# First layer of the experts by eleven block products in place of twelve, with token groups in pairs outside and experts inside

## The chip, the cores and the metric

The kernel runs on one core of a Trainium2 chip. The metric is the device time of one execution in microseconds. A core has five engines that run their own instruction streams in order and wait for each other on semaphores: TensorE (PE, with its weight loads shown as PEld), VectorE (DVE), ScalarE (ACT), GpSimd (POOL) and SyncE (SP, which here only issues DMAs).

## The reference

A delta-rule attention gives x with 3072 tokens and 384 columns. A mixture of 8 experts follows, each a first layer of 384 by 1024, a relu and a second layer of 1024 by 384, weighted per token by P, and last a block of four matrices, two of them side by side with a product by element.

```python
def _moe_ref(x, w_gate, w1, w2):
    ...
    out = np.zeros((N, D), dtype=np.float32)
    for e in range(E):
        h = np.maximum(x @ w1[e], 0.0)
        ye = h @ w2[e]
        out += P[:, e:e + 1] * ye

def _moe2_ref(x, w1, w2, w3, w_out):
    a = x @ w1
    b = x @ w2
    h = a * b @ w3
    return (h @ w_out).astype(np.float32)
```

## The kernel before

All matrices of the mixture and of the last stage are fp32. Each operand is split into a high and a low part, and a product of 128 rows by 128 columns takes three matmuls (high by high, high by low, low by high) that add up in one PSUM bank.

**Order.** The program hands every operation to a class `Plan` with the tiles that it reads and writes, a priority and a cost for each engine that may take it. `Plan` simulates the engines with these costs and so writes one fixed order for each engine; where two engines may take an operation (POOL or DVE for most subtractions) it chooses one. A DMA costs its bytes by 300 GB/s plus 0.9 us there. PSUM banks and buffers are rings that hand out a slot when the last user is done.

**Attention stage.** It runs over 12 chunks of 256 tokens. Expert 0 of a chunk is computed there as well (`e0`), for the first ten chunks.

**Expert stage (`phase_b`).** All 3072 tokens' x, in high and low parts, lie in SBUF (`xT` for five groups of 512 tokens, `xr` for the sixth), and so does `acc`, the weighted sum of all groups. The outer loop runs over 14 half experts (experts 1 to 7, each as two sets of four blocks of 128 hidden columns, after what is left of expert 0), the inner over the six groups. For one half expert and one group PE does 4 blocks x 9 matmuls of 512 columns (first layer, one PSUM bank a block), then 3 x 12 (second layer, one bank for each 128 output columns). ACT writes relu of a block as its high part (L966), DVE the low part with one `scalar_tensor_tensor` (L335), both into a slot of `hA` or `hB`; of these there are five, so that PE may be one block ahead of the second layer. DVE multiplies a second-layer bank by the spread weight `pb` into `tmp` and adds `tmp` to `acc` (L332; POOL may take the sum).

**Weights.** A block of weights (`load_w`, L811) is 384 x 128 of w1 and 128 x 384 of w2, which makes 128 x 768 in a slot of `rawB` (two slots, two DMAs of 192 KB each). ACT copies it to the high part in `wA` (128x768, L325), DVE or POOL subtracts for the low part (128x768, L332). `wA` has eight slots, one for each block of an expert: while one half is used the other is loaded. Since the groups run inside, a set of four blocks is loaded once in six groups.

**Conversion.** The last stage's matrices arrive as 64-bit floats. `convert` turns them into high and low fp32 parts in DRAM (`w_d`), 256 columns a job, in the gaps of the expert stage: six operations on DVE, two on ACT, and one or two that POOL or DVE takes, and DMAs in and out.

**Last stage (`phase_c`).** `xT` is reused: four of its parts for the two first matrices (high and low), the fifth as three slots through which w3 streams, issued on POOL's queue. w3 and w_out are first multiplied with each other (`m34`: 16 pieces of 12 matmuls of 384 columns, each needs 512 KB of w3). Then come 12 chunks of 256 tokens: split of x into high and low (`x2` in `xr`), 16 products of 9 matmuls of 256 columns, the product by element, its split, and 2 x 24 matmuls of 384 columns into the output.

## Time and profile before

| | |
|---|---|
| median of 3 runs | 2250.84 us (2250.38 to 2253.55) |
| the profiled execution | 2248.74 us |
| its span in the trace | 2247.0 us |
| mean granted clock | 0.98 |
| PE busy | 2172.9 us, 97% |
| DVE busy | 1222.3 us, 54% |
| ACT busy | 569.9 us, 25% |
| POOL busy | 187.7 us, 8% |

The span is what the trace covers, from the first to the last instruction; the profiled execution lies 1.74 us above it, the median of the runs 3.84 us. Busy shares are averages over three stages that differ: attention ends near 540 us of the span, the expert stage near 1915 us, the rest is the last stage.

### The profile page before, as it was taken

The numbers are of one execution on the slowest core, as the hardware profiler recorded it, in microseconds if no ns is written. First come the engines' busy times: TensorE is split into PE (matmuls) and PEld (weight loads), VectorE is DVE, ScalarE is ACT, GpSimd is POOL, SyncE is SP. The second block draws the span as 40 slices with busy tenths as digits, with TensorE's granted clock in tenths as the row PEclk, the third lists the DMA queues.
The fourth block names the chain that finished last, engine by engine and source line by source line (L and its number), as shares of the span: only waits on it lengthen the run. The fifth ranks groups of instructions, "written<-read, shape, count | busy, mean of one in ns | idle before, by whom it ended". The sixth has DMA issues, their size and how long they took to land.

```text
span 2247.0 us, 40062 instructions
## 1 busy us (share of the span) xinstructions
PE 2172.9 (97%) x17133; PEld 1900.9 (85%) x17133; DVE 1222.3 (54%) x2147; ACT 569.9 (25%) x1144; POOL 187.7 (8%) x200
## 2 busy tenths in 40 slices
PE   2999999989999999999999999999999999999999
PEld 2999999977888888888888888888888888999999
DVE  8667756768777777776444444444444444223332
ACT  3333233332222222322112121121211111233332
POOL 3000000023211011110000000000000001200000
PEclk6999999999999999999999999999999999999999
DMA  5331232055333232322101010100101043500000
GB/s 193 94 101 57 64 94 61 24 158 171 95 107 111 80 111 86 116 89 85 43 19 43 15 47 15 46 30 28 47 15 32 17 155 85 107 19 15 15 15 22
DMA packets 134691, 153.13 MB, mean 68 GB/s; under 512 B 10608, under 2 KB 105008, under 8 KB 133744
## 3 DMA queue, kind: packets, MB, share of 16 engines
q1 hardware_dynamic: 115632, 128.80, 18.7%
q0 software_dynamic: 18880, 21.76, 3.8%
q8 instruction: 134, 2.20, 0.4%
q14 instruction: 45, 0.37, 0.1%
HBM read 119.23 MB, written 31.29 MB: 67 GB/s over the span
## 4 chain that ended last, share of the span: by engine, by line
PE 91%; DMA 3%; DVE 2%; issue 1%; ACT 1%; POOL 0%; SPq 0%; DVEq 0%; ACTq 0%; POOLq 0%
PE b L321 91%; DMA kt<-in_kT 1%; DMA xs_d<-xst 1%; ACT g L325 1%; DMA xst<-xs_d 0%; POOL wA L332 0%; DVE acc L332 0%; DMA wraw<-in_moe_w 0%; DMA yr<-in_moe_w 0%; DMA pb<-p_d 0%; DMA kraw<-in_k 0%; ACT tt L325 0%; SPq L352 0%; DVE p L335 0%; DVE p L332 0%
## 5 line engine op out<-in xcount | busy, mean ns | idle before, releaser
L321 PE MATMUL b<-xT,wA 128*128 128x512 f32 x2520 | 588.2, 390 | 0.0
L321 PEld LDWEIGHTS b<-xT,wA 128*128 128x128 f32 x2520 | 473.0, 188 | 102.4
L321 PE MATMUL b<-hA,wA 128*128 128x512 f32 (+1 forms) x2304 | 496.1, 357 | 2.2 <-DVE hA L335 1.3
L321 PEld LDWEIGHTS b<-hA,wA 128*128 128x128 f32 x2304 | 383.0, 190 | 70.9 <-DVE hA L335 2.7
L321 PE MATMUL b<-hB,wA 128*128 128x512 f32 (+1 forms) x1584 | 416.2, 390 | 0.0
L321 PEld LDWEIGHTS b<-hB,wA 128*128 128x128 f32 x1584 | 294.2, 189 | 64.4
L332 DVE TENSOR_TENSOR tmp<-b,pb 128x512 f32<-128x512 f32 x252 | 174.0, 691 | 255.4 <-PE b L321 254.6
L966 ACT ACTIVATE hA<-b 128x512 fp32r<-128x512 f32 (+1 forms) x176 | 103.4, 587 | 647.1 <-PE b L321 647.0
L335 DVE SCALAR_TENSOR_TENSOR hA<-b,hA 128x512 fp32r<-128x512 f32 (+1 forms) x216 | 146.8, 680 | 178.2 <-ACT hA L966 166.5
L321 PE MATMUL b<-xr,wA 128*128 128x256 f32 (+1 forms) x1368 | 233.6, 325 | 2.4 <-ACT wA L325 2.1
L321 PEld LDWEIGHTS b<-xr,wA 128*128 128x128 f32 x1368 | 201.7, 191 | 25.0 <-ACT wA L325 2.6
L321 PE MATMUL b<-xr,xT 128*128 128x256 f32 x1728 | 209.9, 283 | 0.0
L321 PEld LDWEIGHTS b<-xr,xT 128*128 128x128 f32 x1728 | 209.3, 192 | 0.0
L335 DVE SCALAR_TENSOR_TENSOR hB<-b,hB 128x512 fp32r<-128x512 f32 (+1 forms) x176 | 119.2, 678 | 151.9 <-ACT hB L966 151.7
L332 DVE TENSOR_TENSOR acc<-acc,tmp 128x512 f32<-128x512 f32 x250 | 180.5, 722 | 6.5
L966 ACT ACTIVATE hB<-b 128x512 fp32r<-128x512 f32 (+1 forms) x176 | 102.9, 585 | 215.8 <-PE b L321 202.2
L332 DVE TENSOR_TENSOR cv<-b,cv 128x256 f32<-128x256 f32 x96 | 40.7, 424 | 163.5 <-PE b L321 162.9
L332 POOL TENSOR_TENSOR wA<-rawB,wA 128x768 fp32r<-128x768 f32 x17 | 36.7, 2157 | 674.9 <-ACT wA L325 674.9
L332 POOL TENSOR_TENSOR cv<-cv 128x256 f32<-128x256 f32 (+1 forms) x68 | 52.5, 772 | 304.0 <-DVE cv L1063 177.4
L325 ACT ACTIVATE cvs<-cv 128x256 fp32r<-128x256 f32 x72 | 29.0, 402 | 167.0 <-DVE cv L335 166.9
L325 ACT ACTIVATE wA<-rawB 128x768 fp32r<-128x768 f32 x56 | 45.8, 841 | 73.6 <-PE b L321 39.9
L321 PE MATMUL b<-wA,hB 128*128 128x384 f32 x288 | 56.5, 337 | 0.0
(137 smaller groups left out, 1783.2 us busy)
## 6 DMA issues: line engine op xcount, KB each, us to landing
pb<-p_d SPq DMA_DIRECT2D x90, 256.0 KB, 3.2
rawB<-in_moe_w SPq DMA_DIRECT2D x112, 192.0 KB, 3.2
w_d<-cvs SPq DMA_DIRECT2D x112, 128.0 KB, 2.5
cvr<-in_w3T SPq DMA_DIRECT2D x32, 256.0 KB, 3.2
xT<-w_d POOLq DMA_DIRECT2D x32, 256.0 KB, 3.4
kt<-in_kT SPq DMA_DIRECT2D x12, 512.0 KB, 5.2
qt<-in_qT SPq DMA_DIRECT2D x12, 512.0 KB, 4.7
cvr<-in_moe_w SPq DMA_DIRECT2D x24, 256.0 KB, 3.2
```

Of the source, the lines that this page charges most:

```text
L321: self.nc.tensor.matmul(*args, skip_group_check=True, **kw)
L325: self.nc.scalar.activation(out=out, in_=in_, func=AF.Copy, **({} if scale is None else {"scale": scale}))
L332: self.E[eng].tensor_tensor(out=out, in0=in0, in1=in1, op=op)
L335: self.nc.vector.scalar_tensor_tensor(out=out, in0=in0, scalar=scalar, in1=in1, op0=op0, op1=op1)
L966: g.op({"ACT": act(N, True)}, lambda e, s=s, h=h, hx=hx, N=N: nc.scalar.activation(out=self.hv(h, hx, N)[:, 0], in_=self.ps(s, N), func=AF ...
```

## The change

The expert stage is turned round. Three passes run outside, each over one pair of token groups (0 and 1, 2 and 3, 4 and 5); inside run the 14 half experts. So there are 42 units of one half expert and two groups. Expert 0 is computed for all 12 chunks in the attention stage.

Within a unit the four blocks are taken in two pairs (`q`). The first layer of a pair of blocks and a pair of groups is a 2 x 2 array of blocks by three blocks of x's columns: 12 block products before. Two of the three columns now go by Winograd's scheme of seven products in place of eight, and the third adds its four: 11 products, 33 matmuls of 512 columns in place of 36. Sums and differences of x blocks (`forms`, nine operands a pass, high and low) are made once a pass; sums and differences of weight blocks are made in every unit by `load_pair`, which takes the place of `load_w`. A pair of blocks is loaded into both slots of `rawB`; ACT copies 768 and 640 columns, DVE or POOL subtracts as many; then five sums of 128 columns are made in place in `rawB`, and 256, 256 and 128 columns of results are copied (ACT) and subtracted (DVE or POOL) into `wS` and the free corner of `wA`. Only then are the two slots free for the next pair. Weights are loaded once for two groups in place of six: 84 pairs, 168 blocks, in place of 56 blocks.

The seven steps of a pair run in three PSUM banks X, Y, Z. After steps 0, 2 and 3 the partial sum in a bank is needed by itself: `hold` has ACT copy it to a buffer `rt` (four slots), while PE goes on adding to the bank or to another. After steps 1, 4 and 5 `done` has DVE add a bank to the held sum, ACT write the relu from `rt` (L1009), and DVE the low part from `rt`. Step 6 goes as all blocks went before, straight from PSUM (L1027). Steps of the two pairs alternate. A second layer of 2 x 3 x 12 matmuls of 512 columns follows, the second group first.

Sums over experts are kept for two groups. They are written to DRAM (`xf_d`) after the first and second pass and read again in the last stage; expert 0's part is added in the unit of expert 4 (`add_first`).

The conversion runs by 128 columns a job (136 jobs in place of 72). The last stage runs by six groups of 512 tokens, in the order 4, 5, 0 to 3, with 9 matmuls of 512 in place of 18 of 256; w3 streams through two, later three, slots in `wS`, and the first group's x goes to `wS` when all of m34 has been done.

```diff
+    def load_pair(self, e_, h, q, prio):
+
+        nc, g, T, a = self.nc, self.g, self.T, self.a
+        r0 = ["w1open", "x11"]
+        n1 = 8 * e_ + 4 * h + 2 * q
+        ps = 2 * h + q
+        raws = []
+        both = {"POOL": pool2(768), "DVE": dve(768)}
+        for j, n in enumerate((n1, n1 + 1)):
+            f, sl = n % 8, n % 8
+            raw = self.rawB.new()
+            raws.append(raw)
...
+            c0 = 128 * j
+            m = 768 - c0
+            g.op({"ACT": act(m)}, lambda e, n=n, rv=rv, c0=c0: self.copy("ACT", self.wb(n)[:, c0:768], rv()[:, c0:768]),
+                 r=[(raw, 0), (raw, 1)], w=[("w", sl, 0)], prio=prio)
+            g.op({"POOL": pool2(m), "DVE": dve(m)}, lambda e, n=n, rv=rv, c0=c0: self.tt(
+                e, self.wb(n)[:, 768 + c0:1536], rv()[:, c0:768], self.wb(n)[:, c0:768].bitcast(F32), ALU.subtract),
...
+        def sub(out, i0, i1, op, m=1):
+
+            g.op({"POOL": pool2(128), "DVE": dve(128)}, lambda e: self.tt(e, k(*out), k(*i0), k(*i1), op), r=[], w=[(r1, 0), (r2, 0)], prio=prio)
...
+        sub((r2, 1), (r2, 0), (r2, 1), ALU.add)
+        sub((r2, 0), (r1, 0), (r2, 0), ALU.subtract)
+        sub((r1, 0), (r2, 1), (r1, 0), ALU.subtract)
+        sub((r1, 1), (r1, 1), (r1, 0), ALU.subtract)
+        sub((r1, 2), (r1, 2), (r2, 2), ALU.subtract)
...
+        for m, src, dst, key in ((256, lambda: T["rawB"][:, r1.at, 0:256], lambda i: ws(i), lambda i: ("wS", ps, i, 0)),
+                                 (256, lambda: T["rawB"][:, r2.at, 0:256], lambda i: ws(i, 256), lambda i: ("wS", ps, i, 1)),
+                                 (128, lambda: T["rawB"][:, r1.at, 256:384], lambda i: self.wb(n1 + 1)[:, 768 * i:768 * i + 128], lambda i: ("w", sl2, i))):
+            g.op({"ACT": act(m)}, lambda e, src=src, dst=dst: self.copy("ACT", dst(0), src()), r=rk + ["bopen"], w=[key(0)], prio=prio)
+            g.op({"POOL": pool2(m), "DVE": dve(m)}, lambda e, src=src, dst=dst: self.tt(e, dst(1), src(), dst(0).bitcast(F32), ALU.subtract),
+                 r=rk + [key(0)], w=[key(1)], prio=prio)
...
+    PASSES = ((0, 1), (2, 3), (4, 5))
...
+            M[-1] += ([("X", [(A11, 3)], True), ("Z", [(A12, 4), (A13, 5)], True), ("X", [(S2, 6)], False),
+                       ("Y", [(S1, 7), (A23, 1)], True), ("X", [(S3, 2)], False), ("Y", [(S4, 8), (S5, 1)], False),
+                       ("X", [(A22, 0), (A23, 5)], False)],)
...
+            def hold(nm, s):
+                t = temps[q, nm] = self.rt.new()
+                g.op({"ACT": act(512, True)}, lambda e: self.copy("ACT", T["rt"][:, t.at], self.ps(s, 512)), r=[s], w=[t], prio=pe)
...
+                g.op({"DVE": dve(512)}, lambda e: self.tt("DVE", tv(), self.ps(s, 512), tv(), ALU.add), r=[s], w=[t], prio=pe)
+                g.op({"ACT": act(512)}, lambda e: nc.scalar.activation(out=hv(0), in_=tv(), func=AF.Relu), r=[t], w=[(out, 0, 0)], prio=pe)
+                g.op({"DVE": dve(512)}, lambda e: self.stt(hv(1), tv(), 0.0, hv(0).bitcast(F32), ALU.max, ALU.subtract),
+                     r=[t, (out, 0, 0)], w=[(out, 1, 0)], prio=pe)
...
+            if step == 0:
+                hold("X1", X)
+            elif step == 1:
+                done("X1", Z, hq["11"])
+            elif step == 2:
+                hold("X2", X)
+            elif step == 3:
+                hold("Y1", Y)
+            elif step == 4:
+                done("Y1", X, hq["22"])
+            elif step == 5:
+                done("X2", Y, hq["12"])
...
+        for idx, (q, step) in enumerate(self.STEPS):
+            product(q, step, idx)
+        for s in (1, 0):
+            bl = [(M[q][3]["12" if s else "11"], M[q][4]) for q in range(2)] + [(M[q][3]["22" if s else "21"], M[q][4] + 1) for q in range(2)]
...
+    STEPS = [(q, s) for ss in ((0, 1), (2, 3), (4,), (5,), (6,)) for q in range(2) for s in ss]
...
-            self.open("xTp", "left", xT=((128, 5, 2, 4, 3, 128), F32R))
-            self.open("accp", "left", acc=((128, 6, 3, 512), F32))
-            self.open("hBp", "right", hB=((128, 5 - HA, 1024), F32R))
-            self.open("cvp", "right", cv=((128, 3, 256), F32), cvr=((128, 2, 512), F32))
-            self.open("cvs", "right", cvs=((128, 2, 256), F32R))
+            self.open("xTp", "left", xT=((128, 4, 2, 4, 3, 128), F32R))
+            self.open("accp", "left", acc=((128, 2, 3, 512), F32))
+            self.open("hBp", "right", hB=((128, HB, 1024), F32R), wS=((128, 4, 1024), F32R))
+            self.open("cvp", "right", cv=((128, 3, CN), F32), cvr=((128, 2, 2 * CN), F32), rt=((128, 4, 512), F32))
+            self.open("cvs", "right", cvs=((128, 2, CN), F32R))
...
-        units = [(0, range(EB, 8))] + [(e_, range(4 * h, 4 * h + 4)) for e_ in range(1, NE) for h in range(2)]
-        for u, (e_, fs) in enumerate(units):
...
+        units = [(p, e_, h) for p in range(3) for e_ in range(1, NE) for h in range(2)]
+        for n, (p, e_, h) in enumerate(units):
...
+            if (e_, h) == (1, 0):
+                self.forms(p, pr - .6)
...
+            if n + 1 < len(units):
+                for q in range(2):
+                    self.load_pair(*units[n + 1][1:], q, pr + .5)
+            self.unit(p, e_, h, pr, 250.0 + n / 100, pb)
+            if (e_, h) == (4, 0):
+                self.add_first(p, pr + .6)
+            if (e_, h) == (7, 1) and p < 2:
+                for s, ch in enumerate(self.PASSES[p]):
+                    self.dma(lambda ch=ch: T["xf_d"][ch], lambda s=s: T["acc"][:, s], 786432, [("acc", s, kk) for kk in range(3)], [("xf", ch)], 260 + n / 100)
...
-        n = 256
+        n = CN
...
-        w3ring = Ring(range(3))
+        w3ring = Ring([0, 1])
+        self.after("ws2", self.last_readers([("wS", 2, i, m) for i in range(2) for m in range(2)]), 2999, hook=lambda end: w3ring.free.append((end, 2)))
...
-        for c in range(12):
...
+        self.after("w3free", self.m34_ops, 2999, hook=lambda end: x2r.free.append((end, 1)))
+        x2 = lambda s, i: (T["xr"].rearrange("p i a h k n -> p (i a h k n)") if s.at == 0 else T["wS"][:, 0:3].rearrange("p a n -> p (a n)"))[
+            :, 1536 * i:1536 * i + 1536].rearrange("p (k n) -> p k n", k=3)
...
+        for ci, c in enumerate((4, 5, 0, 1, 2, 3)):
...
+                    g.op({"PE": 9 * .2267}, ab, r=xk + [k for v in wsrc.values() for k in v[1]], w=[sab[j], (h, "z", j)], prio=pc)
...
-                if full and c < 10:
+                if full:
```

How the order moves at three places. First ACT, in the middle of the expert stage. Before, this is where the copies of a set of weights (`wA<-rawB`, 768 columns) stand among the relus (`hA<-b`, `hB<-b`):

```order
L325 ACTIVATE wA<-rawB 128x768 x2
L1065 ACTIVATE cv<-cvr 128x256
L966 ACTIVATE hA<-b_128 128x512
L966 ACTIVATE hA<-b_130 128x512
L325 ACTIVATE wA<-rawB 128x768
L966 ACTIVATE hB<-b_133 128x512
L325 ACTIVATE cvs<-cv 128x256
L325 ACTIVATE wA<-rawB 128x768
L966 ACTIVATE hB<-b_129 128x512
```

After, in the seventh unit of the first pass, the end of the first layer (`hB<-rt` and `hA<-rt` are relus of held sums, `cv` and `cvs` belong to the conversion):

```order
L327 ACTIVATE wA<-rawB 128x128
L327 ACTIVATE rt<-b_133 128x512
L327 ACTIVATE cvs<-cv 128x128
L1009 ACTIVATE hB<-rt 128x512 x2
L327 ACTIVATE wA<-rawB 128x768
L1009 ACTIVATE hB<-rt 128x512
L327 ACTIVATE wA<-rawB 128x640
L1027 ACTIVATE hB<-b_130 128x512
L1198 ACTIVATE cv<-cvr 128x128
L1009 ACTIVATE hA<-rt 128x512
```

The copies of the second pair of the next unit's weights stand between the last four relus of this unit, and such a group stands in every unit; before it stands once in six groups.

Second DVE, at the same kind of place. Before:

```order
L332 TENSOR_TENSOR wA<-rawB,wA 128x768
L335 SCALAR_TENSOR_TENSOR hA<-b_128,hA 128x512
L335 SCALAR_TENSOR_TENSOR hA<-b_130,hA 128x512
L332 TENSOR_TENSOR wA<-rawB,wA 128x768
L335 SCALAR_TENSOR_TENSOR hB<-b_133,hB 128x512
L332 TENSOR_TENSOR wA<-rawB,wA 128x768
L335 SCALAR_TENSOR_TENSOR hB<-b_129,hB 128x512
```

After, in the thirteenth unit of the first pass (`rt<-b,rt` adds a bank to a held sum; the `rawB<-rawB` sum in the last row belongs to the second pair's weights):

```order
L334 TENSOR_TENSOR rt<-b_130,rt 128x512
L337 SCALAR_TENSOR_TENSOR hB<-rt,hB 128x512
L334 TENSOR_TENSOR rt<-b_131,rt 128x512
L337 SCALAR_TENSOR_TENSOR hB<-rt,hB 128x512
L1192 TENSOR_SCALAR cv<-cvr 128x128
L334 TENSOR_TENSOR wA<-rawB,wA 128x640
L337 SCALAR_TENSOR_TENSOR hA<-rt,hA 128x512
L337 SCALAR_TENSOR_TENSOR hB<-b_134,hB 128x512
L337 SCALAR_TENSOR_TENSOR cv<-cvr,cv 128x128
L337 SCALAR_TENSOR_TENSOR hB<-b_127,hB 128x512
L334 TENSOR_TENSOR rawB<-rawB 128x128
```

Six blocks of a unit have a sum ahead of their low part, and the low parts of the last blocks stand behind a subtraction of the second pair's weights.

Third PE, where the expert stage ends (`wA,xT` and `wA,wS` with 384 columns is m34, `xr,xT` and `wS,xT` the first products of the last stage, `hA`/`hB,wA` the second layer). Before:

```order
L321 MATMUL b_130<-hB,wA 128x512 x3
L321 MATMUL b_133<-wA,xT 128x384 x24
L321 MATMUL b_126<-wA,xT 128x384 x12
L321 MATMUL b_131<-xr,xT 128x256 x9
L321 MATMUL b_132<-xr,xT 128x256 x9
L321 MATMUL b_127<-xr,xT 128x256 x9
L321 MATMUL b_128<-xr,xT 128x256 x9
L321 MATMUL b_126<-wA,xT 128x384 x12
L321 MATMUL b_130<-wA,xT 128x384 x24
```

After:

```order
L323 MATMUL b_127<-hB,wA 128x512 x6
L323 MATMUL b_132<-wA,wS 128x384 x24
L323 MATMUL b_131<-wA,wS 128x384 x24
L323 MATMUL b_134<-wA,wS 128x384 x24
L323 MATMUL b_128<-wA,wS 128x384 x24
L323 MATMUL b_130<-wA,wS 128x384 x24
L323 MATMUL b_133<-wA,wS 128x384 x24
L323 MATMUL b_129<-wA,wS 128x384 x24
L323 MATMUL b_127<-wA,wS 128x384 x24
L323 MATMUL b_132<-wS,xT 128x512 x9
L323 MATMUL b_131<-wS,xT 128x512 x9
```

m34 was mixed with the first products of the last stage and stands now in one piece ahead of all of them.

## Rows read from the trace of the kernel before

**Rows 1.** The page: busy time of the engines over the whole span, and the granted clock of PE in 40 slices.

```profile
PE 2172.9 (97%) x17133; PEld 1900.9 (85%) x17133; DVE 1222.3 (54%) x2147; ACT 569.9 (25%) x1144; POOL 187.7 (8%) x200
...
PEclk6999999999999999999999999999999999999999
```

**Rows 2.** The chain of work that ended last: its last piece (start, us, what), and its shares by line.

```profile
540.67 1702.96 PE b L321 x8419
...
by line: PE b L321 91.5%; issue 1.3%; DMA kt<-in_kT 0.6%; DMA xs_d<-xst 0.6%; ACT g L325 0.5%; DMA xst<-xs_d 0.5%; POOL wA L332 0.4%; DVE acc L332 0.4%; DMA wraw<-in_moe_w 0.4%; DMA yr<-in_moe_w 0.3%; DMA pb<-p_d 0.2%; DMA kraw<-in_k 0.2%; 
```

**Rows 3.** Busy time in three stretches: the expert stage with conversion, the same without, and 10 us in which m34 and the first products of the last stage run. Columns: stretch, its length, busy us (instructions) of PE, PEld, DVE, ACT and POOL, granted clock, share of the DMA engines, GB/s.

```profile
700.00:1000.00 300.00, 300.00 (x1308) 245.05 (x1307) 218.25 (x474) 81.54 (x169) 48.29 (x60) 1.00 0.33 99
1000.00:1300.00 300.00, 300.00 (x1307) 245.10 (x1306) 146.97 (x234) 57.23 (x98) 11.54 (x10) 1.00 0.14 43
...
1920.00:1930.00 10.00, 10.00 (x71) 10.00 (x70) 1.88 (x5) 1.68 (x4) 5.04 (x7) 1.00 1.00 185
```

**Rows 4.** The timeline of PE in the expert stage, one group's turn from the second layer to the first and back. Columns: start us, us, engine, line, operation, tiles, shape, count. A row ends later than the next one begins, since the ends are modelled; a rate is taken from start to start.

```profile
1304.93 1.55 PE L321 MATMUL b<-hB,wA 128*128 128x512 f32 x6
...
1306.32 1.55 PE L321 MATMUL b<-hA,wA 128*128 128x512 f32 x6
...
1308.40 8.37 PE L321 MATMUL b<-xT,wA 128*128 128x512 f32 x36
...
1316.61 0.86 PE L321 MATMUL b<-hB,wA 128*128 128x512 f32 x3
```

**Rows 5.** The timeline of PE at the start of the last stage: m34 (384 columns) and first products (256 columns).

```profile
1906.19 6.41 PE L321 MATMUL b<-wA,xT 128*128 128x384 f32 x36
1912.44 4.47 PE L321 MATMUL b<-xr,xT 128*128 128x256 f32 x36
1916.75 6.41 PE L321 MATMUL b<-wA,xT 128*128 128x384 f32 x36
```

**Rows 6.** The timeline of the other engines around the handover of weights in the part without conversion; in brackets the idle time before an instruction and what ended it.

```profile
1306.55 0.69 DVE L332 TENSOR_TENSOR acc<-acc,tmp 128x512 f32<-128x512 f32 x1
...
1308.19 1.86 POOL L332 TENSOR_TENSOR wA<-rawB,wA 128x768 fp32r<-128x768 f32 x1 [97.43 <-ACT wA L325]
...
1309.33 1.27 DVE L332 TENSOR_TENSOR acc<-acc,tmp 128x512 f32<-128x512 f32 x1
1310.52 0.95 DVE L332 TENSOR_TENSOR wA<-rawB,wA 128x768 fp32r<-128x768 f32 x1
...
1311.50 8.79 SPq L352 DMA_DIRECT2D rawB<-in_moe_w  x8
...
1314.69 0.85 ACT L325 ACTIVATE wA<-rawB 128x768 fp32r<-128x768 f32 x1 [1.36 <-DMA rawB<-in_moe_w]
1315.45 0.58 ACT L966 ACTIVATE hB<-b 128x512 fp32r<-128x512 f32 x1
...
1317.51 0.85 ACT L325 ACTIVATE wA<-rawB 128x768 fp32r<-128x768 f32 x1 [1.48 <-DMA rawB<-in_moe_w]
```

**Rows 7.** The same handover in the part with conversion.

```profile
615.23 0.94 DVE L332 TENSOR_TENSOR wA<-rawB,wA 128x768 fp32r<-128x768 f32 x1
615.48 2.42 POOL L332 TENSOR_TENSOR wA<-rawB,wA 128x768 fp32r<-128x768 f32 x1 [0.73 <-ACT wA L325]
...
616.20 2.64 SPq L352 DMA_DIRECT2D rawB<-in_moe_w  x4
...
620.27 0.85 ACT L325 ACTIVATE wA<-rawB 128x768 fp32r<-128x768 f32 x1 [1.89 <-DMA rawB<-in_moe_w]
...
621.92 0.84 ACT L325 ACTIVATE wA<-rawB 128x768 fp32r<-128x768 f32 x1 [0.33 <-DMA rawB<-in_moe_w]
```

**Rows 8.** Groups of instructions by line, operation and shape: busy us, mean ns of one, idle time before them and what ended it.

```profile
L332 DVE TENSOR_TENSOR acc<-acc,tmp 128x512 f32<-128x512 f32 x250 | 180.5, 722 | 6.5
L332 DVE TENSOR_TENSOR tmp<-b,pb 128x512 f32<-128x512 f32 x252 | 174.0, 691 | 255.4 <-PE b L321 254.6
L335 DVE SCALAR_TENSOR_TENSOR hA<-b,hA 128x512 fp32r<-128x512 f32 x208 | 143.5, 690 | 173.5 <-ACT hA L966 161.7 <-ACT hA L777 10.8
...
L332 DVE TENSOR_TENSOR wA<-rawB,wA 128x768 fp32r<-128x768 f32 x39 | 38.2, 982 | 19.8 <-ACT wA L325 19.7
L332 POOL TENSOR_TENSOR wA<-rawB,wA 128x768 fp32r<-128x768 f32 x17 | 36.7, 2157 | 674.9 <-ACT wA L325 674.9
...
L335 DVE SCALAR_TENSOR_TENSOR cv<-cv 128x256 f32<-128x256 int32 x64 | 27.0, 422 | 2.5
L332 DVE TENSOR_TENSOR cv<-cv 128x256 f32<-128x256 f32 x63 | 26.6, 423 | 10.3 <-POOL cv L332 7.3 <-DVE cv L1063 0.5
L325 ACT ACTIVATE cvs<-cv 128x256 fp32r<-128x256 f32 x64 | 26.5, 414 | 148.9 <-DVE cv L335 148.9
...
L1071 DVE TENSOR_SCALAR cv<-cvr 128x256 int32<-128x256 int32 x64 | 20.8, 324 | 0.0
...
L332 POOL TENSOR_TENSOR cvs<-cv,cvs 128x256 fp32r<-128x256 f32 x26 | 19.6, 755 | 75.4 <-ACT cvs L325 75.4
L332 DVE TENSOR_TENSOR cvs<-cv,cvs 128x256 fp32r<-128x256 f32 x38 | 15.8, 417 | 2.9 <-ACT cvs L325 2.9
...
L332 DVE TENSOR_TENSOR cv<-cv 128x128 f32<-128x128 f32 x13 | 3.8, 292 | 0.8
...
L325 ACT ACTIVATE cvs<-cv 128x128 fp32r<-128x128 f32 x8 | 2.5, 310 | 18.1 <-DVE cv L335 18.0
```

More of the change, by code (lines that the diff above doesn't have):

```diff
@@ L31 @@
 NP = 2
+HB = 7
+CN = 128
 NTC = 2
@@ L883, in phase_b @@
         self.after("x11", [g.wr["xs", 11, b] for b in range(2)], -200)
-        for n in range(EB, 8):
-            self.load_w(n, self.rawB, raw_t, 300, r=["w1open", "x11"])
         def open_b(e):
@@ new lines, in phase_c @@
+        yv = lambda yb: T["yr"].rearrange("p s n -> p (s n)")[:, DM * yb.at:DM * yb.at + DM] if yb.at < 2 else T["tmp"][:, yb.at - 2, 0:DM]
+        for ci, c in enumerate((4, 5, 0, 1, 2, 3)):
+            pc = pr + 20 + ci
+            xb = x2r.new()
+            xs = lambda ci=ci: T["acc"][:, ci % 2]
+            ak = [("acc", ci % 2, kk) for kk in range(3)]
+            if ci > 1:
+                self.dma(xs, lambda c=c: T["xf_d"][c], 786432, [("xf", c)], ak, pc - 1.5)
+            ak = ak + ["x5free"]
+            g.op({"ACT": act(1536)}, lambda e, xb=xb, xs=xs: self.copy("ACT", x2(xb, 0), xs()), r=ak, w=[(xb, 0)], prio=pc)
+            g.op({"POOL": pool2(1536), "DVE": dve(1536)}, lambda e, xb=xb, xs=xs: self.tt(
```

362 lines of the change are left out of this document (198 added, 164 removed).

## The prediction

> **What bounds the kernel now.** I read the page's busy times first, then the chain, then stretches, then single turns. PE is busy for 97% of the span at the granted clock of its upper level, 2.4 GHz, after the first slice [rows 1]. The chain shows that this is no accident of averages: from 540.67 us on it is one piece of PE work of 1702.96 us [rows 2]. In the expert stage PE is busy for 300 of 300 us [rows 3]. So only fewer matmul columns help there, and any wait of PE is paid in full. The second reading is who has room to take on work. With conversion, DVE is busy for 218 of 300 us, without it for 147 [rows 3].
>
> **What leaves PE.** A first-layer matmul takes 8.21 us / 36 = 0.228 us from start to start, a second-layer one 1.39 / 6 = 0.2315 us [rows 4]. Each of 42 units loses 2 x 3 first-layer matmuls: 252 x 0.228 = 57.4 us. In the last stage 1728 matmuls of 256 columns take 4.31 / 36 = 0.1197 us each [rows 5], 206.8 us; as 864 of 512 columns at 0.228 they take 197.0, a gain of 9.8. m34 and the output products keep their columns. All of this lies on the path: **67.2 us**.
>
> **What is added outside the units.** Four terms, 20 us together.
> - m34 was mixed with other products and now runs in one piece. 12 matmuls of it take 6.25 / 36 x 12 = 2.08 us [rows 5] and eat 512 KB of w3; while w3 streams, the DMA engines are full at 185 GB/s [rows 3], so 512 KB take 2.83 us. 16 pieces need 45 us by DMA and 33 us by PE. Two or three pieces lie ready; but the loads of the second matrix (3.1 MB, 17 us by that rate) share the last second layer with them. I take +9, between 3 (all but four pieces hidden) and 16 (nothing ready).
> - The first group's x goes into `wS`, which m34 reads. So an ACT copy and a subtraction of 1536 columns stand between m34 and the next matmul: about twice 0.85 [rows 6] and twice 0.98 us [rows 8], +4 with the handovers.
> - The first unit: its weights must be summed before it starts, while expert 0's last chunks still use DVE and ACT: +3, between 0 and 8.
> - Two changes of pass: 9 copies and 13 DVE or POOL operations of 512 columns. PE's second layer of 72 x 0.2315 = 16.7 us covers them, but DVE has also 6 x (0.69 + 0.72) us of its sums [rows 8] and weights to do in it. +2 each, from 0 to 4.
>
> **What is added in a unit.** This decides the sign. A unit is now 66 x 0.228 + 72 x 0.2315 = 31.7 us of PE work. First the load on DVE, by the mean times of [rows 8]: 6 `tmp` at 0.691, 6 `acc` at 0.722, 6 sums into `rt` priced as `tmp`, 8 low parts at 0.690 give 18.1 us. Weights: the planner gave DVE per unit about 1.4 subtractions of 768 columns (0.98), 0.7 of 640 (about 0.85), 2.8 of 256 (0.417), 1.1 of 128 and 4.7 sums of 128 (0.292): 4.8 us. Conversion: 136 jobs end in the 33rd unit, 4.1 a unit; a job of 256 had three scalar operations near 0.32, two of 0.42 and one tensor operation of 0.42, with the last one for every second job 2.5 us; at 128 columns one of these falls from 0.423 to 0.292, so 1.7 us a job, 7 us. Together **30 of 31.7 us**, where it was 73% before [rows 3]. POOL has about 9 us a unit (2.16 for 768, 0.755 for 256, and by the line through both 0.4 for 128).
>
> In the order fixed by the planner each engine waits for its own head, so what counts is the longest handover. It is the second pair of weights. Both pairs go through the same two slots of `rawB`. Pair one is worked on from the unit's start, since then its slots of `wA` come free: two ACT copies (0.84, 0.75), two subtractions, five sums in place, one behind the other (0.29 each on DVE, 0.4 on POOL), three ACT copies (0.41, 0.41, 0.31) and subtractions, all queued between relus, sums and conversion. Adding these by the two orders, I get the slots free 8.9 us into the unit if no DVE or POOL operation is held up. They are held up, though. An `acc` sum of 0.69 us takes 1.27 when it starts while POOL's subtraction runs, and POOL's 1.86 becomes 2.42 beside DVE's subtraction [rows 6, 7]. With two to four such waits, 0.5 to 0.7 us each, the slots come free at 10.5 to 11.6.
>
> Then the DMAs: first slot released with the subtraction issued at 1310.52 (over at 1311.47), copied from 1314.69; at the next such place, subtraction over at 616.17, copy at 620.27 with conversion's DMAs around [rows 6, 7]. That is 3.2 and 4.1 us; the second slot follows 1.65 us behind the first in [rows 7] and 2.8 in [rows 6], where its own release was later. So the second block lies there about 5.3 us after the release R. From it the path runs to PE: ACT copy 0.75, relu 0.6 of the second pair's block, which stands behind that copy on ACT, then on DVE the subtraction of 640 columns (0.8) and the low part (0.69). PE is at the matmul that needs this block 66 x 0.228 + 3 x 0.23 (one product of the next unit is in front) + 3 x 0.23 = 16.4 us into the unit. **Stall = R + 5.3 + 0.75 + 0.6 + 0.8 + 0.7 - 16.4 = R - 8.3.** R = 8.9 gives 0.6 us, 10.5 gives 2.2, 11.6 gives 3.3. The stall is on PE's path every unit, and nothing catches it up, since the next unit's pair one starts when this second layer ends. Before, such a copy stood ahead of a block's relu only once in six groups, and PE took it without a gap [rows 4, 6].
>
> I take R = 10.5 in the 33 units with conversion, as near to the disturbed rows as to the quiet one, and 9.5 in the 9 without: 33 x 2.2 + 9 x 1.2 = **83 us**.
>
> The Trainium skill, SBUF - State Buffer, section "Who interferes with whom", speaks against this change: a DVE instruction with two SBUF inputs and a GpSimd instruction that reads SBUF exclude each other, and the second fully blocks. The 1.27 us sum agrees. By that rule taken to its end, all 9 us of POOL's work a unit would come on top of DVE's 30, less what falls beside DVE's PSUM work; that is the DVE-bound rival below.
>
> **The sum.** 2247.0 - 67.2 + 20 + 83 = 2282.8 us of span. The profiled run lies 1.74 above its span and the median 2.10 above that, so 2282.8 + 3.8 = **2287 us**, 1.6% slower.
>
> **Rivals.**
> - *The stall stays small (faster).* Mechanism: the second pair's handover. If R is below 9.4, the stall is under (67.2 - 20) / 42 = 1.1 us and the kernel gains. Price at 0.3 us a unit: 2247 - 67.2 + 20 + 13 + 3.8 = 2217; with the outer terms at half, 2207. For it: POOL and ACT have room (ACT 82 of 300 us, POOL 48 [rows 3]), and the conversion's operations on DVE may slip into its waits. Against: two loads for each unit where one in three was enough.
> - *DVE becomes the bound.* If half of POOL's 9 us blocks DVE, a unit with conversion needs 30 + 4.5 = 34.5 us, a stall of 3 to 4 with the handovers: 2247 - 67.2 + 20 + 33 x 4 + 9 x 1.2 + 3.8 = 2346. For it: 30 of 31.7 before any wait. Against: 10 of DVE's 30 us read PSUM and one SBUF tile, and these ran at their usual 0.69 beside POOL.
> - *Stall and gain cancel*, R near 9.4: 2246 to 2255.
> - That fewer matmuls are not issued is excluded by the order: 11 products a pair.
>
> **Chances.** The forecast, stall 1.3 to 3 us a unit with conversion (2258 to 2315): 0.42. DVE-bound or beyond: 0.20. Cancelled, within 0.2% (4.5 us, what a measurement of this kernel can tell from no change): 0.06. Small stall: 0.32. Slower is 0.42 + 0.20 = 0.62. The range runs from the faster rival's 2207 to 2346; what lies below and above has one in ten each. The slower cases alone run from 2258 to 2346.
>
> **What would show it.** In the timeline of the changed kernel PE should stand idle once a unit, in front of its first second-layer matmuls, ended by an ACT relu or DVE low part of `hA` or `hB`; ahead of that relu ACT should wait for the DMA into `rawB`; `rawB`'s DMAs should be issued 10 to 12 us after the unit's start. Units after the 33rd should be shorter by about a us. PE's busy time should be less by some 67 us. m34 should show idle of PE of 5 to 15 us ended by DMAs. I am wrong if PE runs through the second layer without a gap, if the gap is ended by a held sum in the first layer (step 4 waits for the copies in `rt`), or if DVE is busy all the time between the gaps.

## The result and the profile after

The changed kernel takes 2281.18 us (median of 4 runs, 2269.39 to 2285.99), the kernel before in the same comparison 2250.61. The ratio is 1.0129 with an interval of [1.0086, 1.0171]: 1.3% slower, 6 us below the forecast of 2287. The span of the profiled run is 2277.2 us.

The page of the changed kernel, busy times and the two lines of the chain, answers to [rows 1, 2]:

```profile
PE 2148.3 (94%) x16017; PEld 1812.5 (80%) x16017; DVE 1653.9 (73%) x3128; ACT 864.6 (38%) x1795; POOL 568.3 (25%) x682
...
PE 54%; DVE 22%; issue 8%; DMA 7%; ACT 5%; POOL 3%; SPq 1%; DVEq 0%; POOLq 0%; ACTq 0%
PE b L323 54%; DMA rawB<-in_moe_w 4%; DVE wA L334 2%; DVE hB L337 2%; DVE rt L334 2%; DVE hA L337 2%; DVE cv L337 2%; DVE tmp L334 2%; DVE acc L334 2%; DVE rawB L334 1%; SPq L354 1%; ACT wA L327 1%; DVE wS L334 1%; DVE cv L1192 1%; DVE cv L1196 1%
```

PE lost 1116 matmuls, 252 + 864, all that were to go. But the chain, one piece of PE work before, spends 54% of the span on PE and the rest on other engines, DMAs and issue: PE alone no longer sets the pace.

The windows of the changed kernel: first pass, second pass, third pass up to the end of conversion, and the last nine units (columns as in [rows 3]).

```profile
506.36:990.31 483.95, 458.28 (x1929) 362.04 (x1927) 432.07 (x897) 212.85 (x466) 179.54 (x224) 0.99 0.35 101
990.31:1474.81 484.50, 460.01 (x1933) 362.50 (x1932) 434.51 (x889) 210.36 (x458) 179.65 (x224) 0.99 0.32 96
1474.81:1639.99 165.18, 161.94 (x697) 130.11 (x696) 146.67 (x324) 74.52 (x164) 52.03 (x70) 1.00 0.32 96
1639.99:1932.79 292.80, 288.78 (x1235) 232.81 (x1234) 215.16 (x342) 109.86 (x209) 80.76 (x89) 0.99 0.29 86
```

DVE is busy for 89% of the first two passes. PE's own column is to be read with care, though: it shows 458 of 484 us busy, and yet a pass of 14 units needs only 14 x 31.73 = 444 us. A matmul's end is modelled, a short wait in the middle of a row of matmuls partly hides in it, and a matmul at the lower clock counts as busy for longer. The lengths from one unit's first product to the next one's are safer. The 42 units take 1932.79 - 506.36 = 1426.4 us, 33.96 each, which is 93.7 us over 42 x 31.73:

| part | units | over 31.73 us each, in all | forecast |
|---|---|---|---|
| usual units with conversion | 27 | 60.3 us, 2.23 each | 2.2 each |
| usual units without | 7 | 1.7 us, 0.2 each | 1.2 each |
| last unit of passes one and two (38.58, 39.44) | 2 | 14.6 us | 4 and the usual 4.4 |
| the unit that adds expert 0, with the next (39.07 + 29.49, 40.76 + 29.28, 40.88 + 28.14) | 6 | 17.2 us | the usual, 4 x 2.2 + 2 x 1.2 = 11.2 us, nothing more |

Here is one usual unit, from 609.41 to 643.38, in the timeline of the changed kernel:

```profile
609.41 3.58 PE L323 MATMUL b<-xT,wA 128*128 128x512 f32 x15
...
618.45 0.28 DVE L334 TENSOR_TENSOR wA<-rawB,wA 128x128 fp32r<-128x128 f32 x1
...
619.31 1.92 SPq L354 DMA_DIRECT2D rawB<-in_moe_w  x4
...
622.79 0.85 ACT L327 ACTIVATE wA<-rawB 128x768 fp32r<-128x768 f32 x1 [1.73 <-DMA rawB<-in_moe_w]
623.55 0.61 ACT L1009 ACTIVATE hB<-rt 128x512 fp32r<-128x512 f32 x1
624.31 0.74 ACT L327 ACTIVATE wA<-rawB 128x640 fp32r<-128x640 f32 x1 [0.15 <-DMA rawB<-in_moe_w]
624.95 0.62 ACT L1009 ACTIVATE hA<-rt 128x512 fp32r<-128x512 f32 x1
...
623.77 1.85 POOL L334 TENSOR_TENSOR wA<-rawB,wA 128x768 fp32r<-128x768 f32 x1 [6.20 <-DMA rawB<-in_moe_w]
...
624.19 1.98 DVE L337 SCALAR_TENSOR_TENSOR hB<-rt,hB 128x512 fp32r<-128x512 f32 x1 [1.20 <-ACT hB L1009]
...
626.23 0.81 DVE L334 TENSOR_TENSOR wA<-rawB,wA 128x640 fp32r<-128x640 f32 x1
626.97 0.68 DVE L337 SCALAR_TENSOR_TENSOR hA<-rt,hA 128x512 fp32r<-128x512 f32 x1
...
626.23 0.50 PE L323 MATMUL b<-hB,wA 128*128 128x512 f32 x1 [0.66 <-DVE hB L337]
626.57 0.63 PE L323 MATMUL b<-hA,wA 128*128 128x512 f32 x2
627.70 0.50 PE L323 MATMUL b<-hA,wA 128*128 128x512 f32 x1 [0.50 <-DVE hA L337]
```

Read it from below. PE waits in the first products of the second layer, twice, for low parts on DVE. The low part of `hB` takes 1.98 us in place of 0.69, because POOL's subtraction started 0.42 us ahead of it; it starts late in the first place, because its relu stands on ACT behind the copy of the second pair's weights, and that copy waits for a DMA that was issued at 619.31, when the last reader of the slots (618.45) was done. That is the chain the forecast went by. The unit takes 33.97 us, 2.2 over its matmuls, but not all of it here: from start to start of the matmuls, 1.7 us are lost in the second layer and 0.4 in the first.

What ended PE's waits in the 33 units with conversion (us in all, times, longest):

```profile
PE b L323 <- ACT rt L327: 21.3, 25, 4.1
PE b L323 <- DVE hA L337: 18.6, 26, 2.9
PE b L323 <- DVE hB L337: 9.2, 14, 1.3
```

A third kind of wait is the largest single row here: for held sums, in front of step 4, where ACT's copies of weight sums stand ahead of the copies of held banks. ACT in the seventh unit, and PE behind it:

```profile
719.13 0.42 ACT L327 ACTIVATE wS<-rawB 128x256 fp32r<-128x256 f32 x1 [0.48 <-POOL rawB L334]
719.45 0.58 ACT L327 ACTIVATE rt<-b 128x512 f32<-128x512 f32 x1
719.93 0.41 ACT L327 ACTIVATE wS<-rawB 128x256 fp32r<-128x256 f32 x1
720.24 0.59 ACT L327 ACTIVATE rt<-b 128x512 f32<-128x512 f32 x1
...
720.88 1.02 PE L323 MATMUL b<-xr,wS 128*128 128x512 f32 x3 [1.84 <-ACT rt L327]
```

In the 27 usual units with conversion the two places can be parted by the distances from one matmul's start to the next one's: of the 2.23 us a unit, 1.3 lie in the second layer, where the forecast put all of it, and 0.7 in the first layer; the remaining 0.2 lie at neither.

PE in the last stage, from the end of the last second layer:

```profile
1932.79 24.16 PE L323 MATMUL b<-wA,wS 128*128 128x384 f32 x134
1957.13 4.45 PE L323 MATMUL b<-wA,wS 128*128 128x384 f32 x24 [0.18 <-DMA wS<-w_d]
1962.42 6.17 PE L323 MATMUL b<-wA,wS 128*128 128x384 f32 x34 [0.83 <-DMA wS<-w_d]
1970.20 0.50 PE L323 MATMUL b<-wS,xT 128*128 128x512 f32 x1 [1.62 <-ACT wS L327]
1972.00 3.35 PE L323 MATMUL b<-wS,xT 128*128 128x512 f32 x7 [1.29 <-DVE wS L334]
```

m34's 192 matmuls end near 1968.4, 35.6 us for 33.3, so w3's stream costs 2.3 us; the copy and subtraction of x cost 3.5 more.

### The profile page after: what moved, and what is told of

It reads as the page before. It is cut to its first block, busy times and chain, and to the rows that moved or that the text cites. A ratio compares the mean times of both kernels' runs of the same rounds, so it can differ in the third digit from the quotient of the medians.

```text
span 2277.2 us, 41249 instructions
## 1 busy us (share of the span) xinstructions
PE 2148.3 (94%) x16017; PEld 1812.5 (80%) x16017; DVE 1653.9 (73%) x3128; ACT 864.6 (38%) x1795; POOL 568.3 (25%) x682
## 4 chain that ended last, share of the span: by engine, by line
PE 54%; DVE 22%; issue 8%; DMA 7%; ACT 5%; POOL 3%; SPq 1%; DVEq 0%; POOLq 0%; ACTq 0%
PE b L323 54%; DMA rawB<-in_moe_w 4%; DVE wA L334 2%; DVE hB L337 2%; DVE rt L334 2%; DVE hA L337 2%; DVE cv L337 2%; DVE tmp L334 2%; DVE acc L334 2%; DVE rawB L334 1%; SPq L354 1%; ACT wA L327 1%; DVE wS L334 1%; DVE cv L1192 1%; DVE cv L1196 1%
## 5 line engine op out<-in xcount | busy, mean ns | idle before, releaser
L323 PE MATMUL b<-hB,wA 128*128 128x512 f32 x2277 | 587.9, 398 | 9.2 <-DVE hB L337 9.2
L323 PE MATMUL b<-hA,wA 128*128 128x256 f32 (+1 forms) x1611 | 334.2, 338 | 21.1 <-DVE hA L337 19.5
L334 DVE TENSOR_TENSOR rt<-b,rt 128x512 f32<-128x512 f32 x300 | 202.7, 684 | 192.1 <-PE b L323 190.3
L323 PEld LDWEIGHTS b<-hA,wA 128*128 128x128 f32 x1611 | 248.5, 191 | 65.8 <-DVE hA L337 31.7
L334 POOL TENSOR_TENSOR wA<-rawB,wA 128x640 fp32r<-128x640 f32 (+2 forms) x117 | 161.2, 1377 | 389.2 <-ACT wA L327 320.5
L323 PE MATMUL b<-xT,wA 128*128 128x512 f32 x1008 | 250.5, 390 | 0.0
L327 ACT ACTIVATE rt<-b 128x512 f32<-128x512 f32 x300 | 176.4, 592 | 139.2 <-PE b L323 122.2
L323 PEld LDWEIGHTS b<-xT,wA 128*128 128x128 f32 x1008 | 189.1, 188 | 40.7
L327 ACT ACTIVATE wA<-rawB 128x768 fp32r<-128x768 f32 (+2 forms) x252 | 155.7, 624 | 147.1 <-PE b L323 76.4
L323 PE MATMUL b<-xT,wS 128*128 128x512 f32 x756 | 204.8, 397 | 7.0 <-ACT wS L327 2.7
L337 DVE SCALAR_TENSOR_TENSOR hB<-rt,hB 128x512 fp32r<-128x512 f32 x170 | 146.8, 868 | 21.4 <-ACT hB L1009 19.6
L1009 ACT ACTIVATE hB<-rt 128x512 fp32r<-128x512 f32 x170 | 106.3, 629 | 89.4 <-DVE rt L334 87.8
```

The lines of the kernel that those rows point to most:

```text
L323: self.nc.tensor.matmul(*args, skip_group_check=True, **kw)
L327: self.nc.scalar.activation(out=out, in_=in_, func=AF.Copy, **({} if scale is None else {"scale": scale}))
L334: self.E[eng].tensor_tensor(out=out, in0=in0, in1=in1, op=op)
L337: self.nc.vector.scalar_tensor_tensor(out=out, in0=in0, scalar=scalar, in1=in1, op0=op0, op1=op1)
L1009: g.op({"ACT": act(512)}, lambda e: nc.scalar.activation(out=hv(0), in_=tv(), func=AF.Relu), r=[t], w=[(out, 0, 0)], prio=pe)
```

## The experiments

All runs in one table. The ratio is against the kernel before, with its interval; the last column is the mean length of the 42 units from the timeline (PE's matmuls alone need 31.73, and 33.08 in e8). The medians of the kernel before beside these runs went from 2250.61 to 2255.18 us, so a few microseconds between rows say little.

| run | median us | ratio | unit us |
|---|---|---|---|
| the changed kernel | 2281.18 | 1.0129 [1.0086, 1.0171] | 33.96 |
| e1_late | 2232.81 | 0.9913 [0.9896, 0.9929] | 32.86 |
| e5_raw3 | 2263.31 | 1.0043 [1.0029, 1.0058] | 33.46 |
| e2_nopool | 2236.19 | 0.9925 [0.9901, 0.9948] | 32.97 |
| e4_noconv | 2239.34 | 0.9935 [0.9912, 0.9957] | 33.00 |
| e6_spread | 2224.43 | 0.9876 [0.9851, 0.9901] | 32.69 |
| e7_late_nopool | 2209.95 | 0.9802 [0.9786, 0.9817] | 32.31 |
| e9_late_pool | 2297.89 | 1.0194 [1.0176, 1.0212] | 34.39 |
| e8_direct | 2241.57 | 0.9943 [0.9926, 0.9959] | 32.98 |
| e11_swap | 2306.77 | 1.0250 [1.0228, 1.0273] | 34.79 |
| e10_best | 2197.33 | 0.9760 [0.9738, 0.9781] | 31.98 |
| e12_order54 | 2188.35 | 0.9719 [0.9699, 0.9739] | 31.97 |
| e13_swap_noconv | 2262.93 | 1.0051 [1.0028, 1.0073] | 33.49 |

Two theories stood against each other. Theory 1: the stall is the handover of the second pair of weights through two slots, ahead of the second layer. Theory 2: DVE is full, and POOL's blocking fills it further.

**e1_late**, only the planner's idea of a DMA:

```diff
-                     lambda f=f: a["moe_w1"][e_, :, 128 * f:128 * f + 128].rearrange("(k p) f -> p k f", p=128), 196608, r0, [(raw, 0)], prio)
+                     lambda f=f: a["moe_w1"][e_, :, 128 * f:128 * f + 128].rearrange("(k p) f -> p k f", p=128), 196608, r0, [(raw, 0)], prio, lat=2.0)
...
-            self.dma(lambda rv=rv: rv()[:, 384:768], lambda f=f: a["moe_w2"][e_, 128 * f:128 * f + 128, :], 196608, r0, [(raw, 1)], prio)
+            self.dma(lambda rv=rv: rv()[:, 384:768], lambda f=f: a["moe_w2"][e_, 128 * f:128 * f + 128, :], 196608, r0, [(raw, 1)], prio, lat=2.0)
```

> Only the order changes: the planner is told that a weight block's DMA lands 2.0 us later than it assumed, as the trace shows (4.1 us from release to copy, and it reckoned with about 2). It then puts the relus of a unit's last blocks ahead of the second pair's weight copies on ACT. If the handover of the second pair through rawB makes the stall ahead of the second layer (theory 1), 1 to 2 us a unit go and the time is 2215 to 2250. If DVE's load and its waits for POOL make it (theory 2), the order of two copies changes little: 2265 to 2285.

It took 48 us away: 2232.81. The operations and their costs are the same; besides the order only the planner's split between the engines moved a little (203 of the 420 sums of weights on POOL, where it was 224). Nine units now take 31.77 us, PE's own time. The timeline of ACT at the end of such a unit's first layer, and of PE behind it:

```profile
646.58 0.63 ACT L1009 ACTIVATE hB<-rt 128x512 fp32r<-128x512 f32 x1 [1.36 <-DVE rt L334]
647.12 0.30 ACT L1198 ACTIVATE cv<-cvr 128x128 f32<-128x128 uint32 x1
647.33 0.62 ACT L1009 ACTIVATE hA<-rt 128x512 fp32r<-128x512 f32 x1
647.85 0.83 ACT L327 ACTIVATE wA<-rawB 128x768 fp32r<-128x768 f32 x1
...
648.34 0.86 PE L323 MATMUL b<-hB,wA 128*128 128x512 f32 x3
649.04 0.85 PE L323 MATMUL b<-hA,wA 128*128 128x512 f32 x3
```

The relus of held sums stand ahead of the copies, the copy waits for no DMA, and PE goes into the second layer without a gap. The slots come free little earlier than before (the DMAs are issued 9.1 us into this unit, 9.9 in the changed kernel's), and the copies start later, 14.55 us in for 13.38: what helped this unit most is the place of the copies in ACT's order.

**e5_raw3**, a third slot:

```diff
-            self.open("rawp", "right", rawB=((128, 2, 768), F32))
+            self.open("rawp", "right", rawB=((128, 3, 768), F32))
...
-        self.rawB = Ring(range(2), fifo=True)
+        self.rawB = Ring(range(3), fifo=True)
```

> A third slot in rawB, so that the first block of the second pair can be loaded while the first pair is still worked on. Theory 1 (handover): the 1.7 us that ACT waits for that block go, and POOL's subtraction of 768 columns moves out of the way of the last low parts; 2235 to 2262. Theory 2 (DVE's load and locks): the same work on the same engines, 2268 to 2288.

18 us: 2263.31, just outside theory 1's range. PE's waits for held sums rose to 33.2 us over the run, from 21.3: what was saved at one place was partly paid at another.

**e2_nopool**, weights on DVE alone (the same edit at all three places of `load_pair`):

```diff
-            g.op({"POOL": pool2(128), "DVE": dve(128)}, lambda e: self.tt(e, k(*out), k(*i0), k(*i1), op), r=[], w=[(r1, 0), (r2, 0)], prio=prio)
+            g.op({"DVE": dve(128)}, lambda e: self.tt(e, k(*out), k(*i0), k(*i1), op), r=[], w=[(r1, 0), (r2, 0)], prio=prio)
```

> All subtractions and sums of weights on DVE, none on POOL, so that POOL no longer holds DVE up there; DVE gets about 4 us more a unit, 34 for 31.7 us of PE in the units with conversion. If waits between the two engines are the larger part of theory 2, the time falls to 2240 to 2265. If DVE's sheer load is, it rises by 1 to 2.5 us in 33 units: 2300 to 2350. Theory 1 alone: the low part of 640 columns comes earlier than from POOL, the queue on DVE is longer: within 15 us of 2281.

The kernel became 45 us faster, 2236.19, below the ranges of all three cases. But the run did not load DVE as reckoned: it ran 351 more instructions, and its busy time still fell, from 1653.9 to 1640.9 us. Without POOL's weight work beside them its instructions were shorter (the low part from `rt` 722 ns on average for 868), and the planner moved 14 sums into `acc` to POOL. So the run shows that POOL's part of the weight work costs more than it brings here; it doesn't show what a fuller DVE would cost.

**e4_noconv**, the eight operations on DVE and POOL of each conversion job taken out, with an ACT copy in place of the last:

```diff
-            g.op({"DVE": dve(m)}, lambda e, ee=ee, r=r: self.stt(r(), ee(), float(0x38100000), r(), ALU.is_ge, ALU.mult),
-                 r=[(cv, "e")], w=[(cv, "r")], prio=pr)
...
+            g.op({"ACT": act(m)}, lambda e, lo=lo, r=r: self.copy("ACT", lo(), r()), r=[(cv, "r")], w=[(cv, "l")], prio=pr)
```

> Leaves out the arithmetic of the conversion (its DVE and POOL operations; ACT copies raw words to both outputs, the DMAs stay), so the last stage's matrices are not the right ones. DVE loses 7 us a unit in 33 units. Theory 2: the stall falls to the 0.8 us a unit of the units after the conversion, 60 us less: 2210 to 2230. Theory 1: the slots come free about a microsecond earlier, 1.2 to 1.6 us of stall stay: 2235 to 2255.

2239.34, in theory 1's range. Taking out more than a fifth of DVE's work did no more than a better order did with all of it. It did bring 42 us, though, so in the changed kernel's own order DVE's work was not free.

**e6_spread**, with the later DMA, and expert 0 added in six units:

```diff
-            if (e_, h) == (4, 0):
-                self.add_first(p, pr + .6)
+            if e_ in (3, 4, 5):
+                self.add_first(p, pr + .6, 2 * (e_ - 3) + h)
```

> As the run with the later DMA in the planner, and expert 0's part is added in six units (one group and 128 columns each) in place of one: in that run the unit of expert 4 takes 42 us with the one behind it 30, where 31.8 is usual, three times, 24 us in all. If the burst of twelve operations of 512 columns and their loads makes it, 12 to 22 us go: 2210 to 2222. If it is something else of that unit (the middle of the pass), nothing does: 2228 to 2237.

8 us, 2224.43, between the two cases. The long unit is gone (32.42 where it was 41.88), but most of the units that carry a sixth of it lie at 32 to 35 us, and some cost moved there.

**e7_late_nopool**, e6 with e2's edit at the three places:

> The run before this one with all weight arithmetic on DVE. If POOL's blocking still costs time when the order is right, another 5 to 15 us go: 2198 to 2212. If the order alone was the cause, and taking POOL out helped only because it brought the slots of rawB forward, DVE's 4 us more a unit bring nothing or cost up to 10: 2213 to 2228.

Another 14.5 us: POOL's part of the weight work cost time also with the corrected order. The groups by shape show two ways in which it can: in the changed kernel (first fence) and in this one (second), the low part from two SBUF tiles and the weight sums.

```profile
L337 DVE SCALAR_TENSOR_TENSOR hB<-rt,hB 128x512 fp32r<-128x512 f32 x170 | 146.8, 868 | 21.4 <-ACT hB L1009 19.6
L334 POOL TENSOR_TENSOR rawB<-rawB 128x128 f32<-128x128 f32 x224 | 132.9, 596 | 108.7 <-DVE rawB L334 51.9 <-DVE wA L334 41.2 <-issue 4.5
```

```profile
L334 DVE TENSOR_TENSOR rawB<-rawB 128x128 f32<-128x128 f32 x420 | 123.8, 301 | 2.1
L337 DVE SCALAR_TENSOR_TENSOR hB<-rt,hB 128x512 fp32r<-128x512 f32 x170 | 117.3, 700 | 13.7 <-ACT hB L1009 13.4
```

The low part falls from 868 to 700 ns (732 in e6), a weight sum from 596 ns on POOL to 301 on DVE. Five such sums in a chain stand in every handover. How much of the 14.5 us is POOL's blocking of DVE, and how much its own slower sums, no run tells apart. DVE was hardly busier for it: 1639.3 us for 1632.4 in e6.

**e9_late_pool**, the contrary on e6, weights on POOL alone (at the three places):

```diff
-            g.op({"POOL": pool2(m), "DVE": dve(m)}, lambda e, src=src, dst=dst: self.tt(e, dst(1), src(), dst(0).bitcast(F32), ALU.subtract),
+            g.op({"POOL": pool2(m)}, lambda e, src=src, dst=dst: self.tt(e, dst(1), src(), dst(0).bitcast(F32), ALU.subtract),
```

> The same with all weight arithmetic on POOL, which doubles POOL's share and takes 4.8 us a unit from DVE. If DVE's load is the limit it gains: below 2213. If blocking and the handover through rawB are, the slots come free later (a pair is then some 9 us of POOL in a row) and the time rises to 2225 to 2260.

73 us slower than e6, more than expected. PE's waits in its units with conversion are mostly of one kind:

```profile
PE b L323 <- ACT rt L327: 54.9, 41, 2.9
```

**e8_direct**, e6 with twelve products in place of the eleven (cut here to three places):

```diff
-        sub((r2, 1), (r2, 0), (r2, 1), ALU.add)
-        sub((r2, 0), (r1, 0), (r2, 0), ALU.subtract)
...
+                for k in range(3):
+                    wv, j = ws[r][k][0], 3 + k + 3 * s
+                    self.mm(o, wv(0), self.fm(j, 0), start=(k == 0), stop=False)
```

> The new loop order without the seven products: twelve block products a pair of blocks, each in its own bank, no sums of weights or of x, three loads of weights all the same; later DMA in the planner and expert 0 spread as in the first run of this call. The last stage starts a little easier too, since wS is free earlier. PE needs 1.37 us more a unit, 57 us. If the sums and held banks cost nothing any more in the first run of this call, this one is 45 to 60 us slower than that, 2255 to 2280; if they still cost, the distance is smaller, and at 2247 or below the turned loops bring nothing without the seven products and the seven products little.

2241.57, and 40 of its units take 33.07 to 33.09 us: no stall at all. So the turned loops with the new last stage bring about 0.6% by themselves, though weights are loaded three times as often. The seven products are worth 33.08 - 31.73 = 1.35 us a unit, 57 us. The fair partner is e6, which has the same later DMA and spread expert 0: there 17 us of the 57 are left, so their sums and held banks took about 40 back; in e7 32 are left. The changed kernel is 40 us slower than e8, but it also has the planner's short DMA time and expert 0 in one unit, which e8 has not.

**e11_swap**, the changed kernel's own order with one move, made on the finished order:

```diff
+            a, b = min(at[o] for o in cps), max(at[o] for o in self.last_lo[n])
+            moved = []
+            for o in order[a:b + 1]:
+                if o in cps or any(x in moved for x in o.preds):
+                    moved.append(o)
+            rest = [o for o in order[a:b + 1] if o not in moved]
+            order[a:b + 1] = rest + moved
```

> The changed kernel's own order, row for row, with one move: in each unit the two ACT copies of the second pair's raw weights, and the subtractions and whatever hangs on them, stand behind the unit's last low part in place of in front of the last relus. Costs, counts and all other rows are the same. Theory 1 (handover of the second pair ahead of the last relus): some 1.5 to 2 us a unit go in the 27 usual units with conversion: 2225 to 2245. Rival: the run with the later DMA in the planner gained by its other moves (holds, POOL's share, conversion), then this move gives less than half of its 48 us: 2255 to 2278.

A miss in both directions: 2306.77, 26 us slower than without the move. The waits of PE in its 33 units with conversion:

```profile
PE b L323 <- ACT rt L327: 68.7, 51, 5.7
PE b L323 <- POOL wS L334: 1.4, 2, 1.2
```

The waits ahead of the second layer are gone, all 27.8 us of them, and with them all that PE lost there from start to start (48 us in the 33 units of the changed kernel, 0.1 here). So the place of these copies makes that wait. The waits for held sums took their place, 68.7 us for 21.3. The timeline of ACT shows it in the unit that starts at 615.84:

```profile
618.30 1.46 ACT L327 ACTIVATE wA<-rawB 128x768 fp32r<-128x768 f32 x2
...
625.19 0.42 ACT L327 ACTIVATE wS<-rawB 128x256 fp32r<-128x256 f32 x1 [0.50 <-POOL rawB L334]
625.51 0.58 ACT L327 ACTIVATE rt<-b 128x512 f32<-128x512 f32 x1
```

The first pair's copies start 2.5 us after the unit's start, and the copy of a held bank (625.51) stands behind a copy of weight sums that waits for POOL. In the changed kernel the first pair's copies started at 609.03 for a unit that began at 609.41. So the delay that was taken out at the end of the first layer came back a half unit later.

**e13_swap_noconv**, the same move in e4's kernel:

> The move of the run before (second pair's copies behind the last low parts) in the kernel without the arithmetic of the conversion, whose outputs are therefore not the right ones; to be compared with that kernel, 2239. That move took the waits ahead of the second layer away and put longer ones at the held sums in their place. If those come from conversion's operations, which the moved copies push in front of the next unit's first pair on ACT and DVE, they are not there here, and the move gains: 2215 to 2233. If they come from the second pair itself, being done too late for the loop through two slots, they are there without conversion too: 2242 to 2265.

2262.93 against 2239.34: the move costs nearly as much without conversion's arithmetic, and again as waits for held sums (38.2 us against 10.3). So it is not DVE's share of conversion that is pushed ahead. ACT's copies for conversion and their DMAs were still there; whether these or the second pair's own lateness delay the first pair is not told apart.

**e10_best**, e7 with POOL allowed for the first unit's weights (at the three places):

```diff
-            g.op({"DVE": dve(128)}, lambda e: self.tt(e, k(*out), k(*i0), k(*i1), op), r=[], w=[(r1, 0), (r2, 0)], prio=prio)
+            g.op({**({"POOL": pool2(128)} if prio == 390 else {}), "DVE": dve(128)}, lambda e: self.tt(e, k(*out), k(*i0), k(*i1), op), r=[], w=[(r1, 0), (r2, 0)], prio=prio)
```

> The run with later DMA, spread expert 0 and weights on DVE, but for the first unit's weights POOL may help again, since there PE waited 7.9 us for an ACT copy of weights. If that wait comes from DVE working alone on the first unit's weights, 5 to 9 us go: 2200 to 2206. If it is expert 0's last chunks that hold DVE and ACT, nothing: 2207 to 2213.

12.6 us by the medians, more than expected, and 9 by the ratios. The first unit takes 30.97 us where it took 41.98; the units are at 31.98 on average, 0.25 over PE's own time.

**e12_order54**, e10 with group 5 first in the last stage:

```diff
-        for ci, c in enumerate((4, 5, 0, 1, 2, 3)):
+        for ci, c in enumerate((5, 4, 0, 1, 2, 3)):
```

> As that run, with the last stage's groups in the order 5, 4, 0 to 3. Group 5's sum is finished 8 us before group 4's, so its x can go to xr during the last second layer, and its first products can be mixed with m34. If the last stage lost 9 us to m34 alone and 4 us to the copy of x behind it, 8 to 13 us go against the run above. If the load of w3 is the limit whatever stands beside it, only the 4 us of the copy go.

9.0 us: m34 is mixed with the first products again, and PE shows no wait after the last second layer. 2188.35 us, 2.8% below the kernel before, is the best version found.

## Why the prediction was right, step by step

**What leaves PE**: right. The count fell by 252 and 864, and where nothing disturbs, a unit takes 31.77 us (e1, e7) for 31.7 reckoned, the plain products 33.08.

**The stall in a unit**: 2.23 us in 27 units was forecast as 2.2. The chain named is the one in the timeline, and e11 shows that it makes the wait ahead of the second layer. But only 1.3 of the 2.23 us lie there. The slots came free earlier than reckoned: 618.73 - 609.41 = 9.3 us into the unit shown, and the DMAs, forecast at 10 to 12 us, were issued at 9.9 in the median of these units. With R = 9.3 the formula gives 1.0. The end of the chain was longer, because POOL's subtraction held the low part for 1.3 us; the formula had no such term. The other 0.7 us are waits for held sums, which the prediction took as nothing and named only as a sign of being wrong. R too late by 1.2 us and a wait left out cancel: that the total fits to 0.03 us is luck. In the units without conversion it was 0.2 for 1.2, since the slots came free earlier there too: the DMAs were issued 7.8 to 9.3 us into these units.

**What that step did not see**, shown by e11 and e13: the chain is one arc of a loop. A pair goes through slots, ACT, DVE or POOL and back to the slots twice a unit, and the held sums' copies stand in the same queues. Moving the copies took the wait away from where it was forecast and brought a longer one elsewhere. So "R - 8.3" describes one arc of the changed kernel's order and not the loop. What did remove most of the waits was a new order of everything by a planner that knew the DMA's time (e1), or taking POOL's part out of the loop (e2). Why the held sums wait longer when the second pair comes later is read from the order and one timeline; no run takes that wait away alone.

**The terms outside**: 20 us in all was forecast. m34's wait for w3 was 2.3 us in place of 9, the copy of x 3.5 in place of 4. Passes cost more than 4: their last units lie 14.6 us over in place of 4 and the usual 4.4. The start cost nothing: 506.36 + 42 x 31.73 + 335 for the last stage without waits (33.3 of m34, 197 and 101 of products, 3.6 at the end) is 2174, 6 us below 2247 - 67.2. **One term was missing**: the twelve operations that add expert 0 in one unit, with their loads. The six units concerned lie 17.2 us over, of which the usual stall as measured would make 9.4, so the term is worth about 8; spreading it brought 8 as well, in the order of e1 (e6). The misses cancel, which is luck: the sum of 2282.8 for a span of 2277.2 is better than its parts.

**The rivals.** The faster one came about in the reordered kernels: priced at 2217 for a stall of 0.3 us a unit, where e10 has 0.25 and takes 2197, so the terms outside the units were priced too high in it. DVE as the bound did not come about: 2281 and not 2346, and e12 shows that this load alone does not bind, since DVE is busy there for 413.85 of the first 454.82 us of the expert stage, 91%, and a unit lies only 0.24 us over PE's time. POOL's part, its blocking and its slow sums together, is real and was worth 14.5 us (e6 to e7). That a DVE instruction with two SBUF inputs and a GpSimd instruction that reads SBUF shut each other out, as the Trainium skill, SBUF - State Buffer, "Who interferes with whom" has it, fits the trace: 0.69 us became 1.98 beside POOL's 1.85.

**Signs that failed.** PE's busy time was to fall by 67 us; it fell by 24.6, since its records swallow part of the waits and stretches at the lower clock count as busy. m34 was to show 5 to 15 us of idle PE ended by DMAs; it shows 1.0 (0.18 + 0.83), 2.3 by its length. And the wait for held sums, named as a sign of being wrong, stood beside the forecast one: 21.3 us of recorded waits, where both rows ahead of the second layer have 27.8.

## What to carry to other kernels

When an algorithm saves matmuls by sums on other engines, price the longest handover in those engines' fixed orders, and not only their load: here a DVE that is 91% busy was harmless in a good order (e12), and 2 us more for a DMA in the planner brought 48 us. Before giving up on such a change, correct the planner's durations by the trace and plan again; a single operation moved by hand may only move the wait. Try two-input work on DVE alone where GpSimd would share it in a chain, even if DVE is the busier engine (e2, e7); but where DVE is late with such work by itself, as with the first unit's weights, let GpSimd help (e10).
